# Partial DMA sums of tap pairs in the first superblocks of a dynamic convolution with a feed-forward layer

## The chip, the cores and the metric

The kernel runs on one core of a Trainium2 chip. The metric is the device time of one execution in microseconds; the kernel before takes 759.13 us (median of 3 runs, 759.09 to 760.71). Five engines work side by side, each through its own list of instructions: TensorE (PE, with its weight loads as PEld), VectorE (DVE), ScalarE (ACT), GpSimd (POOL) and SyncE (SP), which here only issues DMAs. They wait for each other through semaphores.

## The reference

```python
# x: (8, 4096, 192), weight_gen: (8, 4096, 8 heads, 7 taps)
w = np.exp(weight_gen - max over taps);  w = w / (sum over taps + 1e-09)
x_unf[b, s, k] = x_pad[b, s + k]            # 6 zero rows ahead of each sequence
out = einsum('bshk,bskhg->bshg', w, x_unf)  # 24 channels per head, one weight per head and tap
h = out @ w_in                              # (32768, 192) @ (192, 2048)
result = (h - np.tanh(h)) @ w_out           # (2048, 192)
```

Each token has its own softmax over seven taps for each head. The convolution is a weighted sum of the token's row of x and the six rows before it. A feed-forward layer follows whose nonlinearity is h - tanh(h).

## The kernel before

The 32768 tokens are cut into 32 superblocks of 1024 (128 partitions with J = 8 tokens each); n numbers them from 0.

Softmax of n. SP loads the weights (`load_wg`, L97), ScalarE takes the exponential (`softmax_exp`, L144, without subtracting the maximum), VectorE sums over taps (L155) and takes the reciprocal (L164). The product of both (`scale`, L194) is made by VectorE for later superblocks (`softmax_norm`) and by POOL for 1, 2 and 3.

Products of n (`products`, L220). The seven products of a tap's weight with the shifted x are seven instructions over 128 x 1536 elements, nearly all on POOL. Taps 0, 2, 4 go to the three parts of a tile `even`, taps 1, 3, 5 to those of `odd`, tap 6 to `last`.

Sum over taps. In superblocks 0 to 3 (`PLAIN`) all seven products are added on TensorE. From superblock 4 on POOL issues, after tap 5, a DMA (L235) that adds most of `odd` onto `even`, and TensorE adds what is left: three parts of `even`, `last`, and the third of tap 5 that the DMA left out. `conv_sums` (L268) does the adding and turns channels onto partitions in one go: matmuls of products with an identity matrix, 64 x 64, accumulated in PSUM over the groups in `prods_of`. Each group is 24 matmuls: 16 for the first two thirds of the channels and 8 for the last third. `conv_out` copies the result to `convT` (ScalarE, L286 and L294; VectorE, L292).

First matmul and nonlinearity (`gemm1`, L311): 16 blocks of 128 hidden channels, 6 matmuls each, then tanh on ScalarE (L322) and the subtraction on VectorE (L323) into tiles `gt`. Three PSUM buffers with the tag `ph` go round among these blocks and the convolution's sums.

Second matmul (`gemm2`, L345): for each of 8 token blocks 16 pairs of matmuls. The upper half of the contraction of one block is run with the lower half of the block before; results gather in two banks `obank`, and ScalarE copies them out (L364). The last superblock's blocks are made by `gemm2_last` (L380, L391, L392) with both halves together.

The order of instructions is written out by hand: an engine's list follows the order of the calls in the code. In superblock n the loop over p = 0..7 runs two `gemm1` blocks and one token block of the second matmul of superblock n - 1. The convolution of n + 1 is mixed into token block 6, the products of n + 2 are issued at p = 0, and the softmax of n + 3 is spread over p = 0 to 4. In superblock 1, the exponentials of 3 and 4 both come at p = 0, and the whole sum and reciprocal of 3 (`softmax_norm_ramp`) at p = 1, with the products of 3.

SP's list has the loads of weights, of x and the stores of results, in the order of the calls; it stops at the first one whose buffer isn't free. x has two buffers, so x of n + 3 waits until POOL has made the products of n + 1. `load_x(n + 3)` is called at p = 0 of superblock n, except for n in `LATE` = (1, 2, 3), where it comes at the superblock's end behind the ScalarE copy of the convolution.

At the very end `gemm2(LAST)` runs the lower half of the last block of superblock 30; its first matmul waits for the ScalarE copy of the block before. `gemm2_last` follows for the eight blocks of superblock 31.

Of the kernel before, what the change touches and what calls it, by code (L numbers as in the profile page):

```python
# [8 lines left out]
FP32 = mybir.dt.float32  # L9
# [7 lines left out]
def kernel(  # L17
# [10 lines left out]
    B, S, D = x.shape  # L28
# [7 lines left out]
    J = 8  # L36
# [7 lines left out]
    GC = G // NC  # L44
    NPAIR = K // 2
    ACC = NPAIR * J * D - J * R
    PLAIN = (0, 1, 2, 3)
    assert S % TOK == 0 and D % R == 0 and H * GC == R and F % P == 0
    assert NFT == 2 * J, "one token block of the second matmul per pair of f tiles"

# [90 lines left out]
    def softmax_exp(n):  # L141
# [6 lines left out]
        )  # L148
        e_of[n] = e_t

    def softmax_sum(n, j0=0, j1=J):

        if j0 == 0:
            zsum_of[n] = wgpool.tile([P, J * H], FP32, name="zsum")
        nc.vector.reduce_sum(  # L155
            out=zsum_of[n][:, j0 * H : j1 * H],
            in_=e_of[n][:, j0:j1].rearrange("p j h k -> p (j h) k"),
            axis=AX.X,
        )

    def softmax_recip(n, j0=0, j1=J):
        if j0 == 0:
            zr_of[n] = wgpool.tile([P, J * H], FP32, name="zr")
        nc.vector.reciprocal(zr_of[n][:, j0 * H : j1 * H], zsum_of[n][:, j0 * H : j1 * H])  # L164

    def softmax_norm(n, bank):

        wsm = wgpool.tile([P, J, H, K], FP32, name="wsm")
        zr_v = bank[:, 512 - J * H : 512]
        nc.vector.tensor_copy(zr_v, zr_of[n][:])  # L170
        scale(nc.vector, wsm[:], e_of[n], zr_v)
        wsm_of[n] = (wsm, None, None, None)

    def softmax_norm_ramp(n, bank=None):

        softmax_sum(n)
        wsm = wgpool.tile([P, J, H, K], FP32, name="wsm")
        if bank is None:
            softmax_recip(n)
            wsm_of[n] = (wsm, None, e_of[n], zr_of[n])  # L180
            return
        zr_v = bank[:, 512 - J * H : 512]
        nc.vector.reciprocal(zr_v, zsum_of[n][:])
        if n == 0:
            scale(nc.vector, wsm[:], e_of[n], zr_v)
        else:
            zr_of[n] = wgpool.tile([P, J * H], FP32, name="zr")
            nc.vector.tensor_copy(zr_of[n][:], zr_v)
        wsm_v = bank[:, 0 : J * H * K].rearrange("p (j h k) -> p j h k", j=J, h=H)
        scale(nc.vector, wsm_v, e_of[n], zr_v)  # L190
        wsm_of[n] = (wsm, wsm_v, None if n == 0 else e_of[n], zr_of.get(n))
# [8 lines left out]
    def products(n, taps=None, sums=None, hooks={}, behind=None):  # L200

        x_t = x_of.pop(n)
        wsm, wsm_v, e_t, zr = wsm_of.pop(n)
        if e_t is not None:
            scale(nc.gpsimd, wsm[:], e_t, zr[:])
        in_pairs = n not in PLAIN

        even = ppool.tile([P, NPAIR, NC, J, H, GC], BF16, name="even")
        odd = ppool.tile([P, NPAIR, NC, J, H, GC], BF16, name="odd")
        last = ppool.tile([P, NC, J, H, GC], BF16, name="last")  # L210
        dst = {}
        for i in range(NPAIR):
            dst[2 * i] = even[:, i]
            dst[2 * i + 1] = odd[:, i]
        dst[K - 1] = last[:]
        if -1 in hooks:
            hooks[-1]()
        for eng, k, j0, j1 in taps or [(nc.gpsimd, k, 0, J) for k in range(K)]:
            w = wsm_v if eng is nc.vector else wsm[:]
            mul = eng.tensor_mul(  # L220
                dst[k][:, :, j0:j1].rearrange("p c j h g -> p j h c g"),
                x_t[:, k + j0 : k + j1, :].rearrange("p j (h c g) -> p j h c g", h=H, c=NC),
                w[:, j0:j1, :, k : k + 1]
                .rearrange("p j h (k o) -> p j h k o", o=1)
                .to_broadcast([P, j1 - j0, H, NC, GC]),
            )
            if k == 0 and behind is not None:


                order(mul, behind, "pace")  # L230
            if j1 == 1:
                first_halo[0] = mul
            if k == K - 2 and in_pairs:

                nc.gpsimd.dma_start(  # L235
                    out=even[:].rearrange("p i c j h g -> p (i c j h g)")[:, 0:ACC],
                    in_=odd[:].rearrange("p i c j h g -> p (i c j h g)")[:, 0:ACC],
                    accum_op=mybir.AluOpType.add,
                    max_dma_last_dim=4096,
                )  # L240
            if k in hooks:
                hooks[k]()
        if in_pairs:
            groups = [even[:, i] for i in range(NPAIR)] + [last[:]]
            prods_of[n] = [
                groups + ([odd[:, NPAIR - 1]] if c == NC - 1 else []) for c in range(NC)
            ]
        else:
            prods_of[n] = [[dst[k] for k in (sums or range(K))]] * NC

    def conv_sums(n, parts, pcs, home=None):

# [72 lines left out]

    LAST = (NTOT - 1) * J
    LEAD = 5
    LATE = (1, 2, 3)
    half = {}
    out_of = {}  # L330

# [38 lines left out]
                    in_=out_sb[:],  # L370
                )

    def gemm2_last(j):

        n = NTOT - 1
        po = psum_h.tile([P, 2, HT], FP32, name="po2", tag="ph")
        col = (j % 2) * HT + (j // 2) * P
        for f in range(NFT):
            for r in range(2):
                nc.tensor.matmul(  # L380
                    po[:, r, 0:D],
                    lhsT=g_of[n][f][r * R : (r + 1) * R, col : col + P],
                    rhs=w_out[r * R : (r + 1) * R, f, :],
                    start=(f == 0),
                    stop=(f == NFT - 1),
                )
        if j == 0:
            out_of[n] = opool.tile([P, J, D], FP32, name="out_sb")
        out_sb = out_of[n]
        ot = tpool.tile([P, D], FP32, name="ot", tag="th")  # L390
        nc.scalar.activation(out=ot[:], in_=po[:, 0, 0:D], func=ACT.Copy)  # L391
        nc.vector.tensor_add(out_sb[:, j, :], po[:, 1, 0:D], ot[:])  # L392
        if j % 2 == 1:
            nc.sync.dma_start(
                out=out[n * TOK : (n + 1) * TOK, :].rearrange("(p j) e -> p j e", p=P)[
                    :, j - 1 : j + 1, :
                ],
                in_=out_sb[:, j - 1 : j + 1, :],
            )
# [52 lines left out]
    load_x(1, first_halo[0])  # L452
    load_wg(2)
    softmax_exp(1)

    for c in range(NC):
        nc.scalar.activation(out=w_in[R:P, c, 0:FA], in_=w_in[0:R, c, 0:FA], func=ACT.Copy)
# [14 lines left out]
        for _ in range(m):  # L472
            next(sums, None)

    load_wg(3)
    load_wg(4)
    load_x(3)
    for p in range(J):
        gemm1(0, 2 * p)
        gemm1(0, 2 * p + 1)  # L480


        if p == 3:
            pcs = []
            sums = conv_sums(1, ((0, 1),), pcs, obank)
        if 3 <= p <= 6:
            some(sums, (3 if p == 3 else 1) * 4 * JH)
    some(sums, K * 4 * JH)
# [6 lines left out]
    for n in range(1, NTOT):  # L495
        for p in range(J):
            more = n < NTOT - 1
            if more and p == 6:
                break
            gemm1(n, 2 * p)  # L500
            gemm1(n, 2 * p + 1)
            if p == 0 and n == 1:
                softmax_exp(3)
            if p == 1 and n == 1:
                softmax_norm_ramp(3)
                products(3)
            if n + 3 < NTOT:

                if p == 0:
                    softmax_exp(n + 3)  # L510
                if p == 0 and n + 4 < NTOT:
                    load_wg(n + 4)
                if 1 <= p <= 2:
                    softmax_sum(n + 3, (p - 1) * JH, p * JH)
                if 3 <= p <= 4:
                    softmax_recip(n + 3, (p - 3) * JH, (p - 2) * JH)
            out_block(n, p)
            if p == 0 and 1 < n < NTOT - 2:
                products(n + 2, behind=last_sub[0])
            if p == 0 and n + 3 < NTOT and n not in LATE:  # L520
                load_x(n + 3)
        if not more:
            continue
        gemm1(n, 12)
        gemm1(n, 13)

        pcs = []
        sums = conv_sums(n + 1, ((0, 1),), pcs)
        mix = -(-len(prods_of[n + 1][0]) * 2 * 2 * JH // (NFT - LEAD))
        out_block(n, 6, between=lambda f: some(sums, mix if f >= LEAD else 0))  # L530
        some(sums, K * 4 * JH)
        conv_out(n + 1, ((0, 1),), pcs)
        pcs = []
        some(conv_sums(n + 1, ((2,),), pcs), K * 4 * JH)


        out_block(n, 7, 0, 2)
        conv_out(n + 1, ((2,),), pcs, nc.vector)
        if n + 3 < NTOT:

            softmax_norm(n + 3, pcs[0][:, 0])
        gemm1(n, 14)
        gemm1(n, 15)
        out_block(n, 7, 2)
        if n in LATE:


            load_x(n + 3, last_conv[0])
    gemm2(LAST)
    for j in range(J):  # L550
        gemm2_last(j)


# [28 lines left out]
```

The softmax here doesn't subtract the row's maximum and nothing guards it: scores larger than these inputs give would overflow.

## Time and profile before

| what | value |
|---|---|
| median of 3 runs | 759.13 us |
| profiled execution, its own time | 759.39 us |
| its span from first to last instruction | 757.6 us |
| granted TensorE clock | 0.999 |
| PE busy | 735.7 us (97%), 14848 matmuls |
| DVE busy | 695.7 us (92%) |
| ACT busy | 625.1 us (83%) |
| POOL busy | 668.8 us (88%) |
| DMA | 110.04 MB, mean 145 GB/s |

The profile is of one execution; busy time is the union of an engine's instructions, and the span leaves out what lies ahead of the first and behind the last of them. The chain of work follows back from the last instruction through what released each one, so it names what sets the end. In rows of the timeline the first number is the start, the second the length in microseconds, and brackets hold how long the engine stood idle before it and what ended this. "issue" there means that no semaphore explains the idle time. In the table of waits the numbers are the sum in microseconds, how often, and the longest.

### The profile page before, as it was taken

What the parts mean: (1) busy time and instruction counts of PE and PEld (TensorE: products, weight loads), DVE (VectorE), ACT (ScalarE), POOL (GpSimd) and SP (SyncE); (2) the same over time, 40 slices, a digit from 0 to 9 for tenths busy, and PEclk for the clock granted to TensorE, in tenths of its full rate; (3) what the DMA queues carried; (4) which work ended last, traced back from release to release, by engine and by line L of the source; (5) the groups of instructions that cost most, each with busy time, mean ns of one, the idle gap of its engine ahead of it and who ended that gap; (6) DMA issues with size and microseconds to landing.
All of it is one profiled execution on the core that took longest, in us unless ns stands there. A gap on an engine that the chain in (4) does not pass through costs nothing.

```text
span 757.6 us, 32477 instructions
## 1 busy us (share of the span) xinstructions
PE 735.7 (97%) x14848; PEld 576.2 (76%) x14848; DVE 695.7 (92%) x739; ACT 625.1 (83%) x839; POOL 668.8 (88%) x262
## 2 busy tenths in 40 slices
PE   3899999999999999999999999999999999999997
PEld 2477778777778777777877777777777777877777
DVE  7988899999999999999999999999999999998893
ACT  4887788888888888888888888888888888888882
POOL 8999999999999999999999999999999999999000
PEclk9999999999999999999999999999999999999999
DMA  8903356665555666454666544667544666542212
GB/s 216 239 20 130 132 137 188 172 174 131 142 152 154 185 185 158 117 134 151 181 186 169 116 131 150 174 175 192 111 128 150 169 184 173 120 117 61 76 44 86
DMA packets 25399, 110.04 MB, mean 145 GB/s; under 512 B 4671, under 2 KB 9519, under 8 KB 21294
## 3 DMA queue, kind: packets, MB, share of 16 engines
q1 hardware_dynamic: 14718, 77.03, 28.6%
q0 software_dynamic: 10544, 30.94, 23.8%
q8 instruction: 116, 1.90, 1.0%
q14 instruction: 21, 0.17, 0.1%
HBM read 54.52 MB, written 25.17 MB: 105 GB/s over the span
## 4 chain that ended last, share of the span: by engine, by line
PE 93%; DVE 4%; DMA 1%; ACT 1%; issue 1%; ACTq 0%; DVEq 0%
PE obank L345 43%; PE ph L311 43%; PE pc L268 6%; DVE gt L323 2%; PE po L380 1%; DMA x_t<-in_x_dram 1%; DVE odd L220 0%; ACT th L322 0%; DMA wg_t<-in_weight_gen_dram 0%; DVE zsum L155 0%; DVE even L220 0%; ACT e_t L144 0%; DVE zr L164 0%; DVE wsm L194 0%; ACT convT L286 0%
## 5 line engine op out<-in xcount | busy, mean ns | idle before, releaser
L323 DVE TENSOR_TENSOR gt<-ph,th 128x1024 bf16<-128x1024 f32 x512 | 602.5, 1220 | 35.8 <-ACT th L322 32.2
L322 ACT ACTIVATE th<-ph 128x1024 f32<-128x1024 f32 x512 | 497.3, 1022 | 74.8 <-PE ph L311 71.9
L345 PE MATMUL obank<-w_out,gt 64*128 64x192 bf16 x7936 | 406.9, 243 | 1.2 <-ACT th L322 0.6
L345 PEld LDWEIGHTS <-gt 64*128 64x128 bf16 x7936 | 352.9, 94 | 52.6 <-ACT th L322 0.9
L311 PE MATMUL ph<-convT,w_in 64*128 64x512 bf16 x3072 | 384.1, 378 | 4.8 <-DVE gt L323 2.8
L220 POOL TENSOR_TENSOR even<-x_t,wsm 128x1536 bf16<-128x1536 f32 x93 | 276.6, 2974 | 19.7 <-DVE gt L323 19.5
L220 POOL TENSOR_TENSOR odd<-x_t,wsm 128x1536 bf16<-128x1536 f32 x93 | 276.4, 2972 | 0.0
L311 PEld LDWEIGHTS <-w_in 64*128 64x128 bf16 x3072 | 174.5, 94 | 110.6 <-issue 18.2
L364 ACT ACTIVATE out_sb<-obank 128x192 f32<-128x192 f32 x248 | 82.3, 332 | 35.6 <-PE obank L345 27.8
L220 POOL TENSOR_TENSOR last<-x_t,wsm 128x1536 bf16<-128x1536 f32 x32 | 105.9, 3309 | 0.0
L268 PE MATMUL pc<-ident,even 64*128 64x64 bf16 x2256 | 64.0, 191 | 1.0 <-issue 0.8
L268 PEld LDWEIGHTS <-even 64*128 64x128 bf16 x2304 | 59.8, 96 | 1.8 <-issue 1.0
L235 POOL DMA_DIRECT2D even<-odd x28 | 33.7, 1205 | 8.7 <-POOL odd L220 8.7
L268 PE MATMUL pc<-ident,last 64*128 64x64 bf16 x752 | 27.4, 191 | 9.2 <-POOL last L220 9.2
L294 ACT ACTIVATE convT<-pc 128x1024 bf16<-128x1024 f32 (+1 forms) x33 | 32.7, 993 | 2.6 <-PE pc L268 2.6
L268 PEld LDWEIGHTS <-last 64*128 64x128 bf16 x768 | 23.2, 96 | 9.4 <-POOL last L220 9.2
L292 DVE CAST convT<-pc 128x512 bf16<-128x512 f32 x30 | 20.8, 692 | 6.0 <-PE pc L268 4.0
L155 DVE TENSOR_REDUCE zsum<-e_t 128x32 f32<-128x224 f32 (+1 forms) x60 | 23.5, 392 | 2.9 <-ACT e_t L144 2.9
L144 ACT ACTIVATE e_t<-wg_t 128x448 f32<-128x448 f32 x32 | 18.4, 578 | 6.7 <-DMA wg_t<-in_weight_gen_dram 6.7
L164 DVE RECIPROCAL zr<-zsum 128x32 f32<-128x32 f32 (+1 forms) x58 | 20.3, 350 | 0.1
L194 DVE TENSOR_TENSOR wsm<-e_t,pc 128x448 f32<-128x448 f32 x28 | 17.4, 622 | 2.9
L268 PE MATMUL pc<-ident,odd 64*128 64x64 bf16 x464 | 16.5, 197 | 1.7 <-POOL odd L220 0.7
(28 smaller groups left out, 77.8 us busy)
## 6 DMA issues: line engine op xcount, KB each, us to landing
x_t<-in_x_dram SPq DMA_DIRECT2D x31, 1344.0 KB, 10.9
even<-odd POOLq DMA_DIRECT2D x28, 1024.0 KB, 8.5
out_dram<-out_sb SPq DMA_DIRECT2D x31, 768.0 KB, 6.7
wg_t<-in_weight_gen_dram SPq DMA_DIRECT2D x32, 224.0 KB, 9.8
x_t<-in_x_dram SPq DMA_DIRECT2D x1, 768.0 KB
w_out<-in_moe_w_out_dram POOLq DMA_DIRECT2D x1, 768.0 KB, 10.0
out_dram<-out_sb SPq DMA_DIRECT2D x4, 192.0 KB, 2.2
x_t<-in_x_dram SPq DMA_DIRECT2D x1, 504.0 KB, 6.1
```

What stands on the lines that cost most here:

```text
L155: nc.vector.reduce_sum(out=zsum_of[n][:, j0 * H : j1 * H], in_=e_of[n][:, j0:j1].rearrange("p j h k -> p (j h) k"), axis=AX.X,)
L164: nc.vector.reciprocal(zr_of[n][:, j0 * H : j1 * H], zsum_of[n][:, j0 * H : j1 * H])
L220: mul = eng.tensor_mul(dst[k][:, :, j0:j1].rearrange("p c j h g -> p j h c g"), x_t[:, k + j0 : k + j1, :].rearrange("p j (h c g) -> p j h ...
L235: nc.gpsimd.dma_start(out=even[:].rearrange("p i c j h g -> p (i c j h g)")[:, 0:ACC], in_=odd[:].rearrange("p i c j h g -> p (i c j h g)" ...
L268: nc.tensor.matmul(pc[r][:, col : col + R] if home else pc[:, r, col : col + R], lhsT=prods[c][gi][r * R : (r + 1) * R, c, 2 * j : 2 * j + ...
L292: eng.tensor_copy(out, pc[:, :, 0:cols].rearrange("p r (cj t) -> p r cj t", t=R))
L294: last_conv[0] = nc.scalar.activation(out=out, in_=pc[:, :, 0:cols].rearrange("p r (cj t) -> p r cj t", t=R), func=ACT.Copy,)
L311: nc.tensor.matmul(ph[:, r, :], lhsT=w_in[r * R : (r + 1) * R, c, f * P : (f + 1) * P], rhs=convT[r * R : (r + 1) * R, c, :], start=(c == ...
L322: last_act[0] = nc.scalar.activation(out=th[:], in_=ph_f, func=ACT.Tanh)
L323: last_sub[0] = nc.vector.tensor_sub(gt[:], ph_f, th[:])
L345: mm = nc.tensor.matmul(po[:, 0:D], lhsT=g_of[n][f][r * R : (r + 1) * R, col : col + P], rhs=w_out[r * R : (r + 1) * R, f, :], start=(r == ...
L364: last_act[0] = nc.scalar.activation(out=out_sb[:, j, :], in_=po[:, 0:D], func=ACT.Copy)
```

## The change

- Superblocks 2 and 3 are no longer plain. Superblocks 2 to 5 (`PART`) have a DMA after tap 3 that adds taps 1 and 3 onto taps 0 and 2 (768 KB instead of 1,024 KB); TensorE adds five groups: tap 4, the two sums, tap 5, tap 6.
- From superblock 6 on the DMA is as before, and tap 6 is added first instead of last.
- The weights of 3 are loaded before the copy of the rest of w_in; their exponential comes after the first pair of superblock 0.
- In superblock 1 the sum of 3 is taken in halves at p = 0 and 1, its reciprocal in halves at p = 2 and 3, its products are issued at p = 3; the exponential of 4 comes at p = 2, its sum in halves at p = 4 and 5, its reciprocal behind the last pair ahead of the convolution.
- `LATE` grows to 1 to 6, so x of 7, 8 and 9 are loaded at superblock ends too.
- At the end the first half of the last superblock's first block is issued ahead of `gemm2(LAST)`.

```diff
-    PLAIN = (0, 1, 2, 3)
+    PLAIN = (0, 1)
+    PART = (2, 3, 4, 5)
...
-            if k == K - 2 and in_pairs:
+            if (k, n in PART) in ((3, True), (K - 2, False)) and n not in PLAIN:
+                acc = 2 * J * D if n in PART else ACC
                 nc.gpsimd.dma_start(
-                    out=even[:].rearrange("p i c j h g -> p (i c j h g)")[:, 0:ACC],
-                    in_=odd[:].rearrange("p i c j h g -> p (i c j h g)")[:, 0:ACC],
+                    out=even[:].rearrange("p i c j h g -> p (i c j h g)")[:, 0:acc],
+                    in_=odd[:].rearrange("p i c j h g -> p (i c j h g)")[:, 0:acc],
...
+        if n in PLAIN:
+            prods_of[n] = [[dst[k] for k in (sums or range(K))]] * NC
+        elif n in PART:
+            prods_of[n] = [[dst[4], even[:, 0], even[:, 1], dst[5], last[:]]] * NC
+        else:
+            groups = [last[:]] + [even[:, i] for i in range(NPAIR)]
...
-    LATE = (1, 2, 3)
+    LATE = (1, 2, 3, 4, 5, 6)
...
     softmax_exp(1)
+    load_wg(3)
...
-    load_wg(3)
     load_wg(4)
     load_x(3)
...
+        if p == 0:
+            softmax_exp(3)
...
-            if p == 0 and n == 1:
-                softmax_exp(3)
-            if p == 1 and n == 1:
-                softmax_norm_ramp(3)
-                products(3)
-            if n + 3 < NTOT:
+            if n == 1:
+                if p == 0:
+                    load_wg(5)
+                if p <= 1:
+                    softmax_sum(3, p * JH, (p + 1) * JH)
+                elif p <= 3:
+                    softmax_recip(3, (p - 2) * JH, (p - 1) * JH)
+                else:
+                    softmax_sum(4, (p - 4) * JH, (p - 3) * JH)
+                if p == 2:
+                    softmax_exp(4)
+                if p == 3:
+                    wsm_of[3] = (softmax_tile(), None, e_of[3], zr_of[3])
+                    products(3)
+            elif n + 3 < NTOT:
...
+        if n == 1:
+            softmax_recip(4)
...
+    gemm2_last(0, 0, J)
     gemm2(LAST)
-    for j in range(J):
+    gemm2_last(0, J, NFT)
+    for j in range(1, J):
         gemm2_last(j)
```

`gemm2_last` takes a range of hidden blocks for this and keeps its PSUM tile between the two calls.

More of the change, by code (lines that the diff above doesn't have):

```diff
@@ L149, in softmax_exp, with softmax_tile @@
         e_of[n] = e_t
+    def softmax_tile():
+        return wgpool.tile([P, J, H, K], FP32, name="wsm")
     def softmax_sum(n, j0=0, j1=J):
@@ L166, in softmax_norm @@
     def softmax_norm(n, bank):
-        wsm = wgpool.tile([P, J, H, K], FP32, name="wsm")
+        wsm = softmax_tile()
         zr_v = bank[:, 512 - J * H : 512]
@@ L176, in softmax_norm_ramp @@
         softmax_sum(n)
-        wsm = wgpool.tile([P, J, H, K], FP32, name="wsm")
+        wsm = softmax_tile()
         if bank is None:
@@ L205, in products @@
             scale(nc.gpsimd, wsm[:], e_t, zr[:])
-        in_pairs = n not in PLAIN
         even = ppool.tile([P, NPAIR, NC, J, H, GC], BF16, name="even")
@@ L242, in products @@
                 hooks[k]()
-        if in_pairs:
-            groups = [even[:, i] for i in range(NPAIR)] + [last[:]]
+        if n in PLAIN:
[4 more added lines that the diff above has]
+            groups = [last[:]] + [even[:, i] for i in range(NPAIR)]
             prods_of[n] = [
@@ L247, in products @@
             ]
-        else:
-            prods_of[n] = [[dst[k] for k in (sums or range(K))]] * NC
     def conv_sums(n, parts, pcs, home=None):
@@ L371, in gemm2, with gemm2_last @@
                 )
-    def gemm2_last(j):
+    def gemm2_last(j, f0=0, f1=NFT):
         n = NTOT - 1
-        po = psum_h.tile([P, 2, HT], FP32, name="po2", tag="ph")
+        if f0 == 0:
+            half[j] = psum_h.tile([P, 2, HT], FP32, name="po2", tag="ph")
+        po = half[j]
         col = (j % 2) * HT + (j // 2) * P
-        for f in range(NFT):
+        for f in range(f0, f1):
             for r in range(2):
@@ L386, in gemm2_last @@
                 )
+        if f1 < NFT:
+            return
         if j == 0:
```

## The prediction

> **What bounds the kernel now.** I read the page first, then the chain of work that ended last, the waits, the busy time by stage, and the timeline where a stage is longer than its neighbours. The page and the chain say TensorE nearly everywhere:
>
> ```profile
> span 757.6 us, 32477 instructions
> ...
> PE 93%; DVE 4%; DMA 1%; ACT 1%; issue 1%; ACTq 0%; DVEq 0%
> ...
> q8 instruction: 116, 1.90, 1.0%
> ```
>
> So time is won only by giving TensorE fewer instructions or fewer gaps. I took each superblock's start from its first L311 matmul: 16.62, 37.85, 63.05, 87.44, 110.02, 132.58, 155.51. Superblock 1 thus lasts 25.20 us, 2 lasts 24.39, 3 22.58, 4 22.56, 5 22.93, and 6 to 30 22.57 but for 21 (22.86). The waste is in 1 and 2: 2.63 + 1.82 us over steady state.
>
> Busy time by stage (length, then PE, PEld, DVE, ACT and POOL busy, clock, DMA share, GB/s): rows 1 and 2 are the first six pairs and the convolution of superblock 1, row 3 the convolution of 2, row 4 that of 3, where the DMA has summed the pairs.
>
> ```profile
> 37.85:54.74 16.89, 16.16 (x248) 12.42 (x249) 14.84 (x18) 14.13 (x19) 16.89 (x7) 1.00 0.07 22
> 54.74:60.60 5.86, 5.41 (x221) 4.73 (x218) 4.02 (x4) 3.71 (x6) 5.78 (x3) 1.00 0.01 3
> ...
> 78.83:84.98 6.15, 5.40 (x221) 4.72 (x218) 4.02 (x4) 3.70 (x6) 6.15 (x3) 1.00 0.01 3
> ...
> 103.22:107.55 4.33, 4.33 (x159) 3.74 (x155) 4.01 (x4) 3.08 (x6) 4.33 (x2) 1.00 0.02 4
> ```
>
> The timeline shows the gaps; brackets hold the idle time and what ended it.
>
> ```profile
> 40.59 1.04 ACT L144 ACTIVATE e_t<-wg_t 128x448 f32<-128x448 f32 x2
> ...
> 42.61 1.49 PE L345 MATMUL obank<-w_out,gt 64*128 64x192 bf16 x31 [0.55 <-ACT th L322]
> ...
> 44.86 0.61 DVE L155 TENSOR_REDUCE zsum<-e_t 128x64 f32<-128x448 f32 x1
> 45.57 0.55 DVE L164 RECIPROCAL zr<-zsum 128x64 f32<-128x64 f32 x1
> ...
> 60.01 0.24 PE L268 MATMUL pc<-ident,odd 64*128 64x64 bf16 x5 [0.45 <-issue]
> ...
> 84.28 0.24 PE L268 MATMUL pc<-ident,even 64*128 64x64 bf16 x5 [0.75 <-issue]
> ...
> 92.74 1.24 POOL L235 DMA_DIRECT2D even<-odd  x1 [0.31 <-POOL odd L220]
> ...
> 741.58 1.24 PE L345 MATMUL obank<-w_out,gt 64*128 64x192 bf16 x13 [0.42 <-ACT out_sb L364]
> ```
>
> **A. Softmax of 3 and 4 in superblock 1: +0.60 us.** Pair starts there, from 37.85, are 2.43, 6.01, 8.62, 11.66, 14.27, 16.89; in superblock 3 2.70, 5.32, 7.93, 10.55, 13.16, 15.78. Two steps are long. (1) 2.43 to 6.01: the two exponentials hold ScalarE, the third tanh ends about 42.5 and L345 waits for it. Without them that tanh can start 0.92 us after its matmuls (40.51 less the one that came early, as 47.40 follows 46.48), at about 41.3 instead of 41.53: +0.26. (2) 8.62 to 11.66 is 3.04 against 2.62: the whole sum and reciprocal, 0.61 + 0.55, stand ahead of VectorE's subtractions. As halves of about 0.34 beside pairs of 2.28 they fit 2.62, as they do in superblock 3: +0.42. The exponential of 4 returns at pair 2 and takes the 0.08 that the first step of superblock 3 has over its others (2.70 against 2.62): -0.08. The reciprocal of 4 (0.55) falls where VectorE waited 1.62 us for the convolution's second part.
>
> The exponential of 3 goes into superblock 0 between the second and third tanh. VectorE sets the pace there (subtractions end to end from 19.95, one per 1.146 us); tanh 2 would end at 22.05 and its subtraction starts at 22.24: free, by 0.2 us. The load of weights 3 is moved on SP's queue ahead of the copy of w_in and of x of 2, into DMA time used by the last w_in loads (landed 21.06). Its 224 KB take about 1 us of packets; the copy's packets end at 24.9 and the matmul that reads it starts at 25.87. I take 0, bounds 0 and -0.5.
>
> **B, C. Partial sums of 2 and 3: +1.26 and +1.56 us.** A convolution of seven groups has 168 matmuls, of five 120. Plain against summed, less the issue gap: 5.86 - 4.33 - 0.45 = 1.08 and 6.15 - 4.33 - 0.75 = 1.07 for 64 matmuls, 16.8 ns each; 48 fewer give 0.81. What of the issue gaps? Instructions come in packets of 16384 bytes on q8; 116 x 256 = 29,696 is TensorE's matmuls and weight loads. Counting its instructions (two ahead of the first matmul's pair, one more per superblock from 3), both gaps, and those of superblocks 5 and 21, lie within a few instructions of 192 modulo 256: a block boundary that was reached under 2.7 us after the boundary before. In superblock 1 the boundaries are instructions 62 and 318 of the convolution; with five groups it is over at 280, 318 lies after the next two L311 groups, and the interval grows from 2.23 to some 3.6 us. In superblock 2 they move from 46 and 302 to -114 and 142. So both gaps go: 0.81 + 0.45 and 0.81 + 0.75. Here a page speaks against me: the Trainium skill, "Runtime: NRT & Kernel Launch", section Instruction fetch mechanics, has the sequencer stream blocks on its own, crossings mostly hidden. By it these gaps have another cause and stay: 0.81 and 0.81, sum 2.00. The placement of four gaps on one residue decides for the trace.
>
> The sums' cost lies on POOL: each L235 adds about 1.2 us between products. Superblock 2's last product ends at 54.15 + 1.2 = 55.35, its matmuls begin near 57.5 (convolution from 55.93, last of five groups). Its sum is issued at 45.9 and read at 56.3; that of 3 issued at 68.2 (54.15 + 1.2 + 1.05 + 4 x 2.86 + 0.3), read near 79.2. They move 768 KB; the row of 1,024 KB is
>
> ```profile
> DMA to landing us min/median/max: 8.0/8.5/10.7
> ```
>
> The Trainium skill, "DMA: Bandwidth & Descriptors", section Anatomy of one DMA, gives 2.0 us plus bytes at 436 GB/s: an estimate of 3.8 us for these. The trace is twice that for its own size (4.4 by the page, 8.5 measured), so I take 6 to 8.5. Both fit, by 1.9 us at least.
>
> **D. Four and five take partial sums too: -0.54.** They had four groups and one half (104 matmuls) and get 120: 2 x 16 x 16.8 ns. What it buys: POOL is now 2.4 us later. A full sum of 4 would be issued at 95.1 and land about 103.6; its convolution starts at about 102.2. The partial one is issued at 89.4.
>
> **E. Blocks shifted by 128 instructions: -0.1.** From superblock 5 the boundaries fall where they fell eight superblocks off. Gaps came (0.36, 0.29) where the boundaries were at -5 and -21 from the convolution's start; at -12, -30 and 4 none. Now 6 and 22 have -18, 13 and 29 have -2. About half of the four: -0.7, against +0.65 for the old two; I round to -0.1. Bounds: +0.65 (none) and -1.1 (all four and superblock 3, with -34 in a five-group convolution).
>
> **F. Last superblock: +0.42.** At 741.16 TensorE waits 0.42 for ScalarE's copy. Sixteen matmuls of the last superblock's first block (half of 1.32 us) move into the gap; the PSUM buffer they take was read out by 739.9. None is added.
>
> **x loads of 7 to 9** go from 118.53, 140.09 and 161.65 to superblock ends, 2.6 us before the next start: 127.2, 150, 172.5. POOL reads x of 9 at about 185. At the page's 10.9 us to landing this fits, and queued behind on SP are only weights and stores of the next superblock (behind x of 8 the zero rows, which wait for its landing as they do now). What it could change is the full sum of 6, issued at 135.92 + 2.4 = 138.3 and read, after the group that is now first, at 147.85: 9.5 us. Before it took 10.4 beside an x load issued at 140.09; without that I take 8.5. Cost 0, bounds 0 and -1.2 (at 10.7).
>
> **Sum.** 0.60 + 1.26 + 1.56 - 0.54 - 0.10 + 0.42 = 3.20. The profiled execution took 759.39 us (span 757.6 and 1.8 around it): 756.2. The median is 0.26 lower, so 755.9.
>
> **Rivals.** 1: the issue gaps stay or come back elsewhere (the page's view, or block luck at the lower bound of E): 3.20 - 1.20 = 2.0, so 757.1; with gaps in superblocks 3 and 4 as well, 757.9. For it: the rule; against it: the residue. 2: POOL or the sums are late somewhere in superblocks 1 to 5, since POOL has hardly idle time at first (its waits for VectorE, 19.5 us in all, begin after 200 us): a new wait of TensorE of 1 to 2 us, 757 to 758. 3, slower: the full sum of 6 lands late enough to eat everything. It costs 1 us per us beyond 9.5, so it decides from 12.7 us; with 14.5 the kernel takes 760.9. The longest of 28 was 10.7. 4: the partial sums save no matmuls: excluded, the instruction stream has 64 pairs fewer.
>
> **Chances.** A measurement tells about 0.2% (1.5 us) from no change. Forecast 0.76; rival 1 0.13; rival 2 0.09; rival 3 0.02. All of the forecast, most of 1 and half of 2 lie under 757.6: faster 0.92, same 0.06, slower 0.02. Range: best ends together, E at +0.65 and A a little better, 754.6; worst of w_in (-0.5), E (-1.1) and half of rival 1 reach 757.6.
>
> **What would show it.** Superblock 1 near 23.3 us, 2 near 22.8, 3 and 4 near 22.85; no issue gap at L268 in 1 and 2; pair starts of superblock 1 near 2.4, 5.8, 8.4; L380 ahead of the last L345; 30 rows of L235 for 28. I am wrong if TensorE waits for L235's landing or for POOL in superblocks 1 to 5, if superblock 0 is longer than 21.23 us, or if the gaps gather elsewhere.

## The result

The changed kernel takes 757.11 us (median of 4 runs, 756.82 to 757.46) against 759.76 us of the kernel before in the same rounds (the three runs above and a fourth): ratio 0.9964, 95% interval 0.9947 to 0.9982. A longer measurement later, 21 runs against 25, gave 757.84 against 759.28 us: 0.9979, interval 0.9972 to 0.9985. So the change makes the kernel faster, by 1.4 to 2.7 us. The forecast was 3.2 us and 755.9, range 754.6 to 757.6. The direction came true and the first measurement lies in the range; the size was too large, and the longer measurement lies 0.2 us over the range's upper end.

The page of the changed kernel. TensorE still sets the end, but a stretch of POOL now stands in the chain:

```profile
span 755.1 us, 32326 instructions
...
PE 80%; POOL 17%; DMA 2%; issue 1%; ACT 0%; DVE 0%; POOLq 0%
```

The superblocks' lengths, from first L319 matmul to first L319 matmul, show where the time went (L319 is what was L311; L276 the convolution, before L268; L353 the second matmul, before L345; L240 the DMA sum, before L235):

| stretch | before | after | difference | forecast |
|---|---|---|---|---|
| superblock 0 | 21.23 | 21.08 | -0.15 | 0 |
| 1 | 25.20 | 23.47 | -1.73 | -1.86 (A, B) |
| 2 | 24.38 | 22.78 | -1.60 | -1.56 (C) |
| 3 and 4 | 45.14 | 45.56 | +0.42 | +0.54 (D) |
| 5 | 22.93 | 24.07 | +1.14 | see below |
| 6 and 7 | 45.15 | 45.37 | +0.22 | see below |
| 21 | 22.86 | 22.56 | -0.30 | see below |
| 31 to the end | 37.62 | 37.17 | -0.45 | -0.42 (F) |

The lines of the timeline that answer to those shown of before:

```profile
42.30 1.49 PE L353 MATMUL obank<-w_out,gt 64*128 64x192 bf16 x31 [0.40 <-ACT th L330]
...
138.99 1.20 POOL L240 DMA_DIRECT2D even<-odd  x1 [0.30 <-POOL odd L223]
...
148.97 0.20 PE L276 MATMUL pc<-ident,even 64*128 64x64 bf16 x2 [1.25 <-DMA even<-odd]
...
738.92 0.84 PE L390 MATMUL po<-w_out,gt 64*128 64x192 bf16 x16
...
739.60 1.23 PE L353 MATMUL obank<-w_out,gt 64*128 64x192 bf16 x13
```

The wait for a tanh in superblock 1 is 0.40 instead of 0.55, its second and third pairs start at 5.85 and 8.47 us (6.01 and 8.62 before), and no gap stands before the last L353. The gaps at L268 in superblocks 1 and 2 are gone. A new one is there: in superblock 5 TensorE waits 1.25 us for the full sum of superblock 6.

Busy time by stage of the changed kernel (length, PE, PEld, DVE, ACT, POOL, clock, DMA share, GB/s): from the last pair before the convolution to behind it, for superblocks 1, 2 and 5.

```profile
54.01:58.62 4.61, 4.61 (x174) 4.28 (x172) 4.61 (x6) 3.07 (x6) 4.53 (x3) 1.00 0.02 5
...
76.85:81.39 4.54, 4.54 (x173) 3.97 (x170) 4.02 (x4) 3.00 (x6) 4.54 (x3) 1.00 0.01 4
145.28:151.09 5.81, 4.56 (x159) 4.13 (x155) 4.09 (x4) 3.13 (x6) 5.81 (x3) 1.00 0.21 38
```

Rows 1 and 2 were 5.86 and 6.15 us with 5.4 busy; now TensorE is busy throughout. Row 3 has the wait. So the change won on its path what was forecast and gave 1.5 us back at one place: superblock 5 lost its old gap of 0.36 and is still 1.14 us longer (it is 1.50 us over the steady 22.57, of which the wait is 1.25; where the other 0.25 go was not looked into).

### The profile page after: what moved, and what is told of

It reads as the page before. It is cut to its first block, busy times and chain, and to the rows that moved or that the text cites. A ratio compares the mean times of both kernels' runs of the same rounds, so it can differ in the third digit from the quotient of the medians.

```text
span 755.1 us, 32326 instructions
## 1 busy us (share of the span) xinstructions
PE 734.0 (97%) x14784; PEld 578.5 (77%) x14784; DVE 695.5 (92%) x740; ACT 625.1 (83%) x839; POOL 670.7 (89%) x264
## 4 chain that ended last, share of the span: by engine, by line
PE 80%; POOL 17%; DMA 2%; issue 1%; ACT 0%; DVE 0%; POOLq 0%
PE obank L353 37%; PE ph L319 36%; POOL even L223 7%; POOL odd L223 6%; PE pc L276 5%; POOL last L223 2%; PE po L390 1%; DMA even<-odd 1%; POOL wsm L198 0%; POOL w_in L432 0%; DMA wg_t<-in_weight_gen_dram 0%; POOL even L240 0%; POOL w_out L419 0%; ACT e_t L145 0%; DVE out_sb L404 0%
## 5 line engine op out<-in xcount | busy, mean ns | idle before, releaser
L353 PE MATMUL obank<-w_out,gt 64*128 64x192 bf16 x7936 | 407.7, 243 | 0.4 <-ACT th L330 0.4
L353 PEld LDWEIGHTS <-gt 64*128 64x128 bf16 x7936 | 355.4, 94 | 49.9 <-ACT th L330 0.8
L319 PE MATMUL ph<-convT,w_in 64*128 64x512 bf16 x3072 | 384.8, 378 | 4.7 <-DVE gt L331 2.7
L223 POOL TENSOR_TENSOR even<-x_t,wsm 128x1536 bf16<-128x1536 f32 x93 | 285.1, 3066 | 15.3 <-DVE gt L331 15.0
L223 POOL TENSOR_TENSOR odd<-x_t,wsm 128x1536 bf16<-128x1536 f32 x93 | 284.8, 3063 | 0.0
L319 PEld LDWEIGHTS <-w_in 64*128 64x128 bf16 x3072 | 177.0, 94 | 108.5 <-issue 18.5
L276 PE MATMUL pc<-ident,even 64*128 64x64 bf16 x2256 | 62.9, 191 | 1.5 <-DMA even<-odd 1.2
L276 PEld LDWEIGHTS <-even 64*128 64x128 bf16 x2304 | 59.9, 96 | 2.4 <-DMA even<-odd 1.4
L240 POOL DMA_DIRECT2D even<-odd x30 | 36.1, 1205 | 9.3 <-POOL odd L223 9.3
L276 PE MATMUL pc<-ident,last 64*128 64x64 bf16 x752 | 27.2, 191 | 9.2 <-POOL last L223 9.2
L276 PEld LDWEIGHTS <-last 64*128 64x128 bf16 x768 | 23.3, 96 | 9.4 <-POOL last L223 9.2
L276 PE MATMUL pc<-ident,odd 64*128 64x64 bf16 x400 | 14.4, 199 | 1.2 <-POOL odd L223 0.7
```

The source lines that it names most:

```text
L223: mul = eng.tensor_mul(dst[k][:, :, j0:j1].rearrange("p c j h g -> p j h c g"), x_t[:, k + j0 : k + j1, :].rearrange("p j (h c g) -> p j h ...
L240: nc.gpsimd.dma_start(out=even[:].rearrange("p i c j h g -> p (i c j h g)")[:, 0:acc], in_=odd[:].rearrange("p i c j h g -> p (i c j h g)" ...
L276: nc.tensor.matmul(pc[r][:, col : col + R] if home else pc[:, r, col : col + R], lhsT=prods[c][gi][r * R : (r + 1) * R, c, 2 * j : 2 * j + ...
L319: nc.tensor.matmul(ph[:, r, :], lhsT=w_in[r * R : (r + 1) * R, c, f * P : (f + 1) * P], rhs=convT[r * R : (r + 1) * R, c, :], start=(c == ...
L353: mm = nc.tensor.matmul(po[:, 0:D], lhsT=g_of[n][f][r * R : (r + 1) * R, col : col + P], rhs=w_out[r * R : (r + 1) * R, f, :], start=(r == ...
```

## The wait of superblock 5: experiments

My theory from this profile: two things come together there. POOL issues the sum of 6 late, 3.1 us after its old time of 135.92, and the sum takes 9.9 us to land. In the DMA packet records 15 of its 16 completions are written by 146.65. The sixteenth comes at 147.84, behind a 16 KB instruction packet for TensorE that runs from 146.90 to 147.85. The sum's last data packet had ended at 146.92. The records do not name the engine of a packet; that this one and the completion share an engine is inferred from the times. Rival: lateness alone; the sum takes what it takes.

**Partial sum for superblock 6 too.**

```diff
-    PART = (2, 3, 4, 5)
+    PART = (2, 3, 4, 5, 6)
```

> Edit: superblock 6 takes the partial sum too. Both theories of the 1.25 us wait in superblock 5 (POOL's backlog makes the full sum of 6 late; or an instruction block of TensorE delays its last completion) expect the wait gone here, because the sum is issued 5.7 us earlier, near 133.3. Superblock 5 should take 22.8 us instead of 24.07, 16 matmuls more (0.22) being in that. The full sum of 7 comes first then: issued at 160.5, read near 170.5; if it takes 9.2 us as now, no wait. Total about 1.2 us less than the changed kernel, near 755.9. If a wait of 0.5 us or more turns up in superblock 6 instead, the backlog is the cause and only moves on.

Measured: superblock 5 takes 22.78 us, nothing waits in superblock 6, the time is 756.36 us (ratio to before 0.9956, 0.9941 to 0.9971). The stage of superblock 5 in this kernel:

```profile
146.50:151.00 4.50, 4.50 (x170) 3.86 (x168) 3.80 (x6) 3.14 (x5) 4.50 (x2) 1.00 0.01 4
```

The wait is cured by 5.7 us of lead. This does not tell the theories apart. Superblock 8 took 0.4 us longer, at a gap without a semaphore. The same kernel, measured beside the changed one:

> Superblock 6 with the partial sum, again, in the same rounds as the changed kernel: superblock 5 at 22.78 us without a wait, the time 0.6 to 1.3 us below the changed kernel's of the same rounds.

756.69 us (5 runs; ratio to before 0.9967, 0.9955 to 0.9980) against 757.84 us: 1.15 us below the changed kernel, and superblock 5 takes 22.84. Only three of the changed kernel's 21 runs are as low as the highest of these five (757.10), so this version is the fastest of the three.

**The changed kernel again, twice.**

> The changed kernel unaltered, a second look beside the kernel with superblock 6 in partial sums. If the wait of superblock 5 belongs to the kernel and not to one execution, it is there again, between 0.5 and 1.5 us, and the sum of 6 is issued again 3.1 us later than before the change (near 139.0). If it was chance, superblock 5 takes 22.6 to 22.8 us. Time near 757.1.

> The changed kernel unaltered, a third look. The wait of superblock 5 should be 1.2 to 1.3 us once more, superblocks 1 to 4 at 23.47 and 22.78 us. If the timed runs that lie above the first profiled one lose their time in the ramp (TensorE's clock granted late or taken back in superblock 0), or at block crossings after superblock 5, one of the two differs here from the first look.

The first of them:

```profile
149.03 0.20 PE L276 MATMUL pc<-ident,even 64*128 64x64 bf16 x2 [1.27 <-DMA even<-odd]
```

The sum was issued at 139.00, and the instruction packet came at 146.96. The median of this measurement, 757.84 us, is 0.7 above the expected 757.1. In the other the packet came 7.6 us after the issue instead of 7.9, the sum took 9.6, the wait is 1.01 us, 0.2 less than expected, and superblock 5 takes 23.68 us. Both things named in its expectation differ: superblock 0 took 21.35 instead of 21.08, and superblock 13 took 23.08 at a gap. Superblocks 1 to 4 are 23.47 and three times 22.78 in all three profiles. The wait belongs to the kernel.

**Moving TensorE's instruction blocks.** Extra matmuls at the very start, 108 and 36 of them (`EXTRA`), shift where a block of 256 instructions ends.

```diff
     ctx.enter_context(tc.manual_schedule())
...
+    idle = psum_h.tile([P, 2, HT], FP32, name="idle", tag="ph")
+    for i in range(EXTRA):
+        r = i % 2
+        nc.tensor.matmul(
+            idle[0:R, r, 0:R],
+            lhsT=ident[r * R : (r + 1) * R, r * R : (r + 1) * R],
+            rhs=ident[r * R : (r + 1) * R, r * R : (r + 1) * R],
+            start=True,
+            stop=True,
+        )
```

> Edit: the changed kernel with 108 more small matmuls at TensorE's very start, while it waits for the first product; their result is read by nobody. They shift TensorE's blocks of 256 instructions by 216. Theory 1: the sum of 6 landed late because the 16 KB instruction packet of 146.90 to 147.85 sat ahead of the last of its 16 completions; shifted, that packet comes about 1 us later, the sum lands by 147.5 (8.5 us after its issue) and the 1.25 us wait of superblock 5 goes: 22.6 us instead of 24.07, total near 755.9. Theory 2: the sum is late because POOL issues it late, whatever TensorE's blocks do: it lands 9.9 us after its issue again, wait 1.25, total near 757.1.

Measured: the sum lands 8.6 us after its issue and superblock 5 has no wait (22.49). The time is 758.05 us instead of 755.9. In the profiled execution the ramp (the stretch up to the end of superblock 0) was worse: the first L319 came at 18.15 instead of 16.62, superblock 0 took 21.94, and superblock 7 took 0.8 us longer at a gap of 0.64. That is also why this run is weaker than meant. TensorE was 2.4 us later in superblock 5 and POOL only 1.6, so with 9.9 us the wait would have been about 0.4, not 1.25.

> Edit: the changed kernel with 36 more small matmuls at TensorE's very start; their result is read by nobody. Blocks are shifted by 72 instructions: in superblock 1 the boundaries fall at -10 and 246 of the convolution and in superblock 4 at -26 and 230. If a gap follows from two boundaries met within some 2.7 us, a gap of 0.2 to 0.5 us appears in superblock 1 (23.47 to about 23.8) and perhaps in 4. The instruction packet near 146.9 comes about 1.7 us earlier, in the middle of the sum of 6; one of the 16 DMA engines then loses 0.95 us and the sum lands 9 to 9.4 us after its issue, wait in superblock 5 0.4 to 0.7 us instead of 1.25. If block positions don't matter, all superblocks keep their times.

Measured: the sum lands 9.1 us after its issue, as expected with the packet in its middle. The expected wait of 0.4 to 0.7 us did not come, for TensorE was 2.4 us later here too and POOL 1.2; even a sum of 9.9 us would have been waited for by less than 0.1. The expected gap in superblock 1 did not come either (23.47), nor one in 4: two block boundaries 2.5 us apart are not enough by themselves.

Both landings (8.6, 9.1) speak for the packet. Lateness alone had said 9.9 both times. The closest comparison is in a kernel described further down, whose softmax and tail are as before. There the sixteenth completion was written at 7.94 us after the sum's issue, the packet began at 7.94 as well, and the sum landed at 8.4. In the changed kernel the packet began at 7.91, the completion was written at 8.85, behind it, and the sum landed at 9.9.

A count points the same way. It takes the full sums in all 14 traces of this study and asks whether a packet of instructions, for TensorE or another engine, was under way between a sum's first packet and its landing. The 93 sums with none took 7.98 us in the median (half of them between 7.95 and 8.01, all but seven 9.0 or less). The 214 with exactly one took 9.14 (8.41 to 9.43), and the 63 with two or three 9.3. So both theories hold a part. At 7.98 us the sum would have landed at 147.0, at 8.4 us at 147.4, both ahead of its reader at 147.72; and with the old issue time it would have been early even with 9.9 us. The count does not explain the slowest landings: 20 sums, all of superblocks 6 to 12, took 11.0 to 13.2 us. In the changed kernel TensorE waited for none of them.

**Loads of x back at p = 0.**

```diff
-    LATE = (1, 2, 3, 4, 5, 6)
+    LATE = (1, 2, 3)
```

> Edit: the changed kernel with x of 7, 8 and 9 loaded at p = 0 of superblocks 4, 5 and 6 again. If the load beside a sum is what the late loads avoid, x of 8 starts near 143, during the sum of 6, which lands 10.4 to 11 us after its issue at 139.0, so near 149.7; the wait of superblock 5 grows from 1.25 to about 2 us, and the sum of 7 in superblock 6 takes 10.7 instead of 9.2. If the loads don't bear on the sums, superblock 5 stays at 24.07.

Measured: superblock 4 takes 24.74 us instead of 22.78, superblock 5 23.71, one run 759.1 us. The sum of 6 took 8.6 us and TensorE, 2 us later, did not wait for it, so neither expectation was right. What lengthens superblock 4 is this line, no wait for a sum:

```profile
130.33 0.81 PE L319 MATMUL ph<-convT,w_in 64*128 64x512 bf16 x5 [1.78 <-issue]
```

It stands at a block boundary. The instruction packet for it came at 127.93, after x of 7, issued at 121.60; in the changed kernel, where this load is issued at 127.73, the packet came at 125.31. The load's last packet ended at 127.93 too, just when the instruction packet began. That the load held the packet back is what these times suggest, in a single execution; the kernel before has its load at this place as well and no gap there. In superblock 5 there is another gap, of 0.89 us; its packet, at 149.72, came while x of 8 was being moved.

**Full sums for 4 and 5.**

```diff
-    PART = (2, 3, 4, 5)
+    PART = (2, 3)
```

> Edit: only superblocks 2 and 3 take the partial sum; 4 and 5 have the full one, as before the change. By the prediction's part D the full sum of 4 is issued near 95.9, lands near 104.4 and is read near 102.0, so TensorE waits about 2.4 us in superblock 3, which then takes near 25.0 us instead of 22.78; superblocks 4 and 5 have no wait, since TensorE is later by then. Rival: the sums of 4 and 5 would have been in time and the partial ones only cost 0.22 us each: superblock 3 at 22.57 and superblock 4 at 22.57.

Measured: superblock 3 takes 28.00 us, 5.2 more than with the partial sum, and the one run 760.65 us. The wait:

```profile
105.93 0.20 PE L276 MATMUL pc<-ident,even 64*128 64x64 bf16 x2 [3.78 <-DMA even<-odd]
```

The sum was issued at 95.9 as computed, but took 10.0 us, with an instruction packet at 103.85 near its end. The rest is TensorE's clock, in the stages from the wait on (columns as above):

```profile
102.10:105.90 3.80, 0.05 (x4) 0.00 (x0) 1.96 (x2) 0.49 (x1) 3.80 (x3) 1.00 0.34 58
105.90:107.50 1.60, 1.57 (x52) 1.56 (x54) 0.00 (x0) 0.00 (x0) 1.60 (x1) 0.67 0.00 0
107.50:109.40 1.90, 1.90 (x64) 1.89 (x60) 0.05 (x1) 1.23 (x2) 1.90 (x2) 0.50 0.05 9
109.40:112.00 2.60, 2.60 (x42) 1.73 (x40) 1.94 (x4) 1.52 (x3) 2.60 (x2) 0.91 0.58 157
```

After 3.78 us of idling the granted clock is 0.50 from 106.4 to 109.9, and the convolution that follows takes some 1.6 us longer. So part D bought more than it was priced at: the partial sums of 4 and 5 cost 0.42 us and avoid this.

## The gaps and the parts of the change: experiments

**The kernel before with its blocks moved.** The same extra matmuls, 64 of them, in the kernel before.

> Edit: the kernel before with 64 more small matmuls at TensorE's very start; their result is read by nobody. That shifts the blocks by 128 instructions. If the issue gaps of superblocks 1 and 2 (0.45 and 0.75 us) are block crossings met too soon, boundaries move from 62 and 318 of the convolution to -66 and 190, and from 46 and 302 to -82 and 174, both gaps go, superblock 1 takes 24.75 instead of 25.20 and superblock 2 23.64 instead of 24.39, and the kernel is about 1.2 us faster with 128 instructions more. If crossings are hidden and the gaps belong to the convolution's length, both stay and the time is that of before.

Measured: superblock 1 24.57 instead of 25.20, superblock 2 23.47 instead of 24.39: both gaps are gone. From the table of waits:

```profile
PE pc L268 <- issue: 0.4, 1, 0.4
```

It was 1.4 us in 3 waits. The one that is left is in superblock 13, where a block boundary has come to 13 instructions ahead of the convolution. The profiled execution gained the expected 1.2 us in its span (756.4 against 757.6): 0.6 and 0.9 in superblocks 1 and 2 and 0.6 from old gaps in 5 and 21 that did not come, less 0.5 lost in the ramp and 0.5 in superblock 13. The medians show less, 758.95 us against 759.31 (ratio 0.9992, 0.9983 to 1.0), 0.4 us; where the timed runs lose the rest stays open.

**Superblocks 2 and 3 on TensorE again.**

```diff
-    PLAIN = (0, 1)
-    PART = (2, 3, 4, 5)
+    PLAIN = (0, 1, 2, 3)
+    PART = (4, 5)
```

> Edit: the changed kernel with superblocks 2 and 3 summed on TensorE alone, 4 and 5 with the partial sum. By part B superblock 1 has its 48 matmuls and the boundaries 62 and 318 back: 0.81 + 0.45 over 23.47, so 24.7 us; superblock 2 near 24.3. POOL is 3.2 us earlier, so the sum of 6 is issued near 135.9 and superblock 5 has no wait: 22.6. Total about 1.2 us more than the changed kernel.

Measured: superblock 1 24.98, superblock 2 24.39, superblock 5 22.49 without a wait; one run, 759.31 us, 1.5 to 2.2 more than the two medians of the changed kernel. For the wait of superblock 5 this shows little, since POOL issued the sum 2.8 us earlier, but TensorE was 4.1 us later as well. The gaps are back at the same groups as before the change:

```profile
59.99 0.24 PE L276 MATMUL pc<-ident,odd 64*128 64x64 bf16 x5 [0.77 <-issue]
...
84.26 0.24 PE L276 MATMUL pc<-ident,even 64*128 64x64 bf16 x5 [0.75 <-issue]
```

In superblock 1 the gap is 0.3 larger than before, so 24.98 instead of 24.7. Superblocks 3 and 4 took 23.29 and 22.92, 3 with a gap of 0.34 at L353 at a block boundary; not expected. The sum of 6 was issued at 136.2 and took 11.0 us, without harm.

**Softmax and tail as before the change.**

```diff
-        if p == 0:
-            softmax_exp(3)
...
-                if p <= 1:
-                    softmax_sum(3, p * JH, (p + 1) * JH)
...
+            if p == 0 and n == 1:
+                softmax_exp(3)
+            if p == 1 and n == 1:
+                softmax_norm_ramp(3)
+                products(3)
...
-    gemm2_last(0, 0, J)
     gemm2(LAST)
```

> Edit: the changed kernel with the exponentials of 3 and 4, the sum and the reciprocal of 3 where they were before (superblock 1, pairs 0 and 1), and with the last superblock's first block in one piece behind the last L353; the rest as changed. By parts A and F superblock 1 takes about 0.6 us more than 23.47, so 24.07, all of it ahead of its convolution, and the last superblock's end comes 0.42 later from its start (37.17 to 37.6 us). If the time of superblock 1 was won by the fewer matmuls and the gap alone, it stays at 23.47.

Measured: superblock 1 takes 23.98 (+0.51), and the end comes 37.76 us after the start of superblock 31 instead of 37.17 (+0.59; 37.62 before the change). The lines of before are there again, shifted by this run's later ramp:

```profile
42.31 1.04 ACT L145 ACTIVATE e_t<-wg_t 128x448 f32<-128x448 f32 x2
...
44.32 1.49 PE L353 MATMUL obank<-w_out,gt 64*128 64x192 bf16 x31 [0.55 <-ACT th L330]
...
46.57 0.61 DVE L159 TENSOR_REDUCE zsum<-e_t 128x64 f32<-128x448 f32 x1
...
741.70 1.24 PE L353 MATMUL obank<-w_out,gt 64*128 64x192 bf16 x13 [0.42 <-ACT out_sb L372]
```

Parts A and F are worth what they were priced at, within 0.2 us. Its time of 759.64 us says little: the ramp was 1.9 us longer, with the clock at half from 23.9 to 27.3, and superblocks 6 and 13 took 0.5 and 0.9 us longer at gaps.

**The kernel before, unaltered.**

> The kernel before unaltered, a second look. If the gaps of superblocks 1, 2, 5 and 21 follow from block positions, they are at the same instructions: 25.2, 24.4, 22.9 and 22.9 us. If the ramp's clock differs from execution to execution whatever the kernel, the first matmul of superblock 0 or its length (21.23) differs here too.

Measured: 25.24 and 24.11 us in superblocks 1 and 2, with gaps of 0.50 and 0.48 at the same instructions. But superblocks 5 and 21 have none (22.57 each), and 28 has one (23.13), whose boundary lies at -12. The position makes a gap possible; whether it comes differs from one execution to the next. The ramp was like the first (16.68 and 21.09).

All 14 traces together settle what these gaps are. After the ramp they have 21 gaps of TensorE over 0.15 us that no semaphore explains. Counted in matmuls, weight loads and semaphore instructions, every one stands at 192 or 193 modulo 256, also in kernels whose counts the edits had shifted. In every one the last instruction packet for TensorE had ended 1.2 to 1.6 us before TensorE went on: it had been waiting for its instructions. Mostly it does not have to: 1,572 boundaries were passed. For 55 of them there were under 2.7 us from the first matmul behind one boundary to the last ahead of the next, and 15 of these have a gap, among them all six under 2.35 us, which are those of superblocks 1 and 2. The other six gaps came after longer intervals (3.1 to 5.9 us), so something else made their packets late; the load of x above is the one candidate that was seen.

## Why the prediction was right or wrong

**A, B, C, F: right.** Superblocks 1 and 2 gave 1.73 + 1.60 = 3.33 us where 3.42 were forecast (A alone 0.58 of 0.60, by the start of the seventh pair, 16.31 us instead of 16.89), the tail 0.45 for 0.42. The step that a rule spoke against held. The Trainium skill, "Runtime: NRT & Kernel Launch", section Instruction fetch mechanics, calls the cost of crossing a block mostly hidden. As a rule that agrees with the count, 21 gaps at 1,572 boundaries; but taken for these two gaps it would have left them in place and the gain at 2.0 us, and moving the blocks took both away, in one profile, while three profiles with the old count have both (before twice, and superblocks 2 and 3 on TensorE again). The count of positions was right. The threshold that I put on it, 2.7 us, was not: most boundaries met within it have no gap, such as the pair at 2.5 us above.

**D: right in sign and a little too dear** (0.42 for 0.54). What it avoids was understated: 5.2 us at superblock 3 where I computed a wait of some 1.4 (3.8 of wait, most of the rest the clock).

**x loads and the full sum of 6: the step that failed.** It was costed at 0 with bounds to -1.2 and came to -1.5 (22.57 to 24.07). That is more than the whole miss against the first profile, 0.7 us. Two figures were off. I put 2.4 us of delay on POOL for two L235 (1.2 each, the length of its row). The trace of before had the right figure, in the row of 92.74 and the next two:

```profile
114.34 1.22 POOL L235 DMA_DIRECT2D even<-odd  x1 [0.30 <-POOL odd L220]
...
135.92 1.20 POOL L235 DMA_DIRECT2D even<-odd  x1 [0.30 <-POOL odd L220]
```

Between the first two issues lie 21.60 us; less seven products of 2.86 that leaves 1.58 for one. Two of them make 3.2, and the sum was issued 3.07 us later, at 138.99, not 138.3: 8.73 us ahead of its reader instead of 9.5. And I took 8.5 us to landing because no x load ran beside it. None did, yet it took 9.9, since TensorE's own instruction packet fell on its end. Either error alone would have cost less: with the late issue and 8.5 us the sum lands at 147.5, in time; with the early issue and 9.9 us at 148.2, a wait of 0.5.

Two rivals named this. The second, a new wait of 1 to 2 us somewhere in superblocks 1 to 5 because POOL or the sums are late, 757 to 758 us, is what happened, and so is the first sign I gave of being wrong, that TensorE waits for L235's landing there. I gave it 0.09. The third stood at exactly this sum; its mechanism came true, at less than half of the size from which it would have decided. The 10.7 us that I took for the longest landing was the longest of one execution: the second profile of the kernel before has one of 12.8. The range left the bound of -1.2 out, too: its upper end was put together from w_in, E and half of rival 1, which by their figures make some 758.0, not 757.6. That the first measurement lies inside owes something to luck.

**The late x loads, costed at 0,** seem to be worth about 2 us in superblock 4, in a single execution, where the load ran up to the instruction packet. That was no step of mine.

**E: -0.1 was forecast; the first profile has about +0.4.** The gaps of 5 (0.36) and 21 (0.30) went, and 6, 7 and 14 show 0.3 together. That is luck: the second profile of the kernel before lacks these two gaps without any change, and in other profiles of the changed kernel 7 and 13 lose 0.3 to 0.5 us. The boundaries were placed right (a recount in the trace has them at -18 in 6 and 22 and at -2 in 13 and 29), but what would come of them was a guess. In the three profiles of the changed kernel 6 lost 0.1 us once, 13 lost 0.1 and 0.5, and 22 and 29 nothing. And 7, where the boundary lies 94 instructions into the convolution, was not on the list, though it lost 0.1 to 0.5 us in all three.

**The sum of what the first profile shows:** 3.33 + 0.45 - 0.42 - 1.50 + 0.38 + 0.15 (superblock 0) = 2.4 of the 2.5 between the spans, 757.6 and 755.1. The 0.15 goes with the ramp's clock, full from 22.0 us on before and from 21.1 after; other executions of the changed kernel do not have it (21.33, 21.35), so it is no merit of the change. Between 2.5 and the 1.4 us of the longer measurement something stays open. The three profiled executions of the changed kernel (756.88, 757.36, 757.11) lie in the lower part of its timed runs (756.48 to 758.92), those of before (759.39, 758.88) in the lower half or the middle of theirs. Longer ramps, as three of the variants show them, and more gaps at block crossings would do it; no profile shows an execution from the upper part of that range.

## What to carry to other kernels

Take the price of an instruction that issues a DMA from the distance between the issues around it, not from the length of its row: here 1.58 us against 1.20. Where a transfer must land ahead of a reader, compare the slack with its slow landings over several executions, not with the median of one. TensorE's instructions came by DMA too (queue q8), and one 16 KB packet of 0.95 us ahead of the last of 16 completions made a sum of some 8.4 us one of 9.9. Gaps that no semaphore explains and that all stand at one residue of the instruction count are block crossings. What helped here was fewer instructions in the dense stretch, or a shift of the count; but every edit ahead shifts all of them.

## What the runs showed that I had not expected

- A full sum takes 7.98 us in the median without an instruction packet beside it and 9.14 with one, over 307 of them. Where the packet fell on the last completion, 9.9 and 10.0.
- TensorE waited for its own instructions: at all 21 gaps that no semaphore explains, its packet had ended 1.2 to 1.6 us before. An x load in front of such a packet went with a gap of 1.78 us.
- One wait of 3.78 us halved TensorE's clock for 3.4 us and so cost another 1.6. The waits of 1.0 to 1.3 us and the gap of 1.78 left it at 1.00. This agrees with the Trainium skill, "TensorE: Matmul & The Clock Gate", section Why this matters for your kernels, which warns of idle gaps over some 3 us.
- The ramp differs from execution to execution: full clock for good from 19.3, 20.1 and 21.1 us on in the three profiles of the changed kernel, from 27.1, 27.3 and 27.5 in three variants, with superblock 0 between 21.1 and 22.5 us. That is as much as the change is worth, so edits of this size had to be read by stages, not by the total.
